# Two mixer layers on one core: bulk transfers of the second attention issued by GpSimd, and its last visits written out in a fixed order with row sums taken in the residual add

## The chip, the core and the metric

The kernel runs on one core of one Trainium2 chip. The time is the device time of one execution in microseconds (us); a kernel is timed in several runs and the median counts. A core has TensorE (PE, matrix products; PEld are its weight loads), VectorE (DVE), ScalarE (ACT), GpSimd (POOL) and SyncE (SP). Each engine works through its own queue of instructions in order and waits on semaphores for the others. TensorE writes its results to eight PSUM banks, each of 128 partitions by 512 fp32 numbers; everything else lies in SBUF, or in HBM, from and to which transfers (DMAs) run. An engine that issues a DMA only starts it, and the transfer lands later.

## The reference

Four blocks in a row, attention, token MLP, attention, token MLP, with the same weights in both rounds:

```python
    x = A_x                                            # [1, 2048, 1024], bf16
    x = x + _A_ref(_layernorm(x, axis=-1), A_wqkv, A_wo)
    x = x + _B_ref(_layernorm(x, axis=-1), B_w1, B_b1, B_w2, B_b2)
    x = x + _A_ref(_layernorm(x, axis=-1), A_wqkv, A_wo)
    x = x + _B_ref(_layernorm(x, axis=-1), B_w1, B_b1, B_w2, B_b2)
```

`_A_ref` is local dilated attention: 32 heads of 32 columns; each token attends to itself and the seven tokens before it at a distance of 2, 4, ..., 14:

```python
        qkv = x @ wqkv                                 # split into q, k, v per head
        off = jnp.arange(8) * 2
        idx = pos[:, None] - off[None, :]              # only idx >= 0 counts
        logits = jnp.einsum("bhsd,bhswd->bhsw", q, kg) * scale
        attn = softmax(where(mask, logits, -1e9))
        o = jnp.einsum("bhsw,bhswd->bhsd", attn, vg)
        return o @ wo
```

`_B_ref` is an MLP over tokens: `gelu(h^T w1 + b1) w2 + b2` with `w1` of 2048 x 3584, and `_layernorm` subtracts the row's mean and divides by the root of its variance.

## The kernel before

**Layout.** Tokens of even and odd number never attend to each other, so they are two classes c = 0, 1 of 1024 tokens, each in eight tiles i of 128. `order` lists the 16 tiles (c, i), class 0 first. `x` is kept as rows in DRAM (`xa`, `xb`), one row tile of 128 x 1024 bf16 (256 KB) per (c, i).

**The second attention** is the part that the change touches. Its q and k projections use seven products for the eight of a 2 x 2 block product (the "sevens" of the change's name, class `Attention`). One step p (there are `NP` = 8, p = 0 to 7) makes k and q for 128 columns (four heads) of one class; the weights are cut into eight blocks of 512 KB, and their sums into as many more. Before the steps, `QkBlocks` scales the blocks and forms the sums, and `keep` (L526) writes both to DRAM (`sdq`), two 512 KB stores per block; the blocks of steps 0 and 1 are used straight from SBUF (`take`). `load` (L567) reads one block and its sums back, two DMAs of 512 KB.

A step's work is given as one string per engine (L535 to L538): `P1k` ... `P7q` are the seven products for k and for q, each of four matmuls (L651); `c11q`, `c21q` (ScalarE, L712) and `y12q`, `y22q` (VectorE, L713) write the four quarters of q. `dc11q`, `dy12q`, `dy22q`, `dc21q` copy these quarters, four DMAs of 32 KB each (L667), into the padded tiles `qB`, in which each head has its own columns. `wk` and `wq` load the weights of a later step, or near the end a half of wo (`load_wo`, L742); `wx` is what is done once in a certain step: the stores of the last two blocks in step 1 (`keep_last`), the first three residual rows in step 6 (`first_rows`, through `load_xr`, L901). A name that ends in `-` belongs to the step before. `cycle` merges the strings into one program, so that each engine's order is that of its string; `chain_` fixes that order. Before the change all of these DMAs are issued by SP, in the order `dc21q- wx wk wq dc11q dy12q dy22q`.

**Visits.** Alongside step p run four visits of the attention proper over the columns of step p - 1 (16 blocks of work times two halves of tokens make 32 visits): scores `S` (L799), exp `e` on ScalarE (L807), four masks `m` that multiply the exponentials of a quarter of the partitions by a band into `Pm` (L823), values and row sums `V` (L848, L852, L861), the reciprocal in two ScalarE steps (L866, L869), and the divide `n` into `oT` (L874). The values of a visit come two visits after its scores. `V` uses two PSUM banks ("a"), which fall free with the divide.

**Output projection.** `out_proj` (L903) makes one row tile: two halves of eight matmuls (L912) in the two banks "m", on VectorE an add of the residual row for each half (L919), a store of the row, and a layer norm in three pieces (`ln_a`, `ln_b`, `ln_c`): two `bn_stats` (L930), their aggregate (L934), on ScalarE the root as a logarithm and an exponential (L208, L209), on VectorE the bias (L938), and on ScalarE the normalisation into `h2` (L952). `ln_step` issues one piece at a time after a half.

**The end of the second attention.** After the eight steps come the last visits: the rest of step 7, then four visits (`vis` from `2 * NU - 4`), in which SP, VectorE and TensorE are interleaved with `last_tile`, seven tiles in all. There, masks 2 and 3 of a visit are given to GpSimd and masks 0 and 1 to VectorE:

```python
                in_order(scores, *divmod(vis, 2))
                chain_("POOL", lambda: mask(2, 3, eng=nc.gpsimd))
                chain_("DVE", mask, 0, 1)
```

The remaining nine tiles follow in a plain loop, and then the MLP (`gemm1`; its first matmuls are L993). Its first work is on GpSimd, 32 sums and differences of `h2` tiles (`token_sums`, L1007), in the order of the tiles.

**Pools.** `wp` (nine buffers) holds weights, `gop` (14 buffers) holds `oT`, q, k, their sums and the residual rows, `vhp` (16 buffers) holds `v` and then `h2`, `x2p` (six) short-lived tiles.

Of the kernel before, what the change touches and what calls it, by code (L numbers as in the profile page):

```python
# [17 lines left out]
P = 128  # L18
# [10 lines left out]
def kernel(  # L29
# [139 lines left out]
    civ = const.tile([P, 2], FP32, name="civ")  # L169
    mx0 = const.tile([P, NPRE, DIL, NI // 2], FP32, name="mx0")  # L170
# [332 lines left out]
    class QkBlocks:  # L503
# [22 lines left out]
        def keep(self, n):  # L526
            r, t = self.R.pop(n), self.S.pop(n)
            chain_("SP", lambda: nc.sync.dma_start(out=sdq[n][0], in_=r[:].bitcast(FP16)))
            chain_("SP", lambda: nc.sync.dma_start(out=sdq[n][1].rearrange("p k c -> p (k c)"), in_=t[:].rearrange("p a k c -> p (a k c)")))

    class Attention:
# [4 lines left out]
        SP = "dc21q- wx wk wq dc11q dy12q dy22q"  # L536
# [30 lines left out]
        def load(self, phi):  # L567
            n = 2 * TURN[phi // 2 % (NG // 2)] + phi % 2
            ts = [wp.tile([P, KD, 256], FP16, name="Aq", tag="w"), wp.tile([P, 4, 4, P], FP16, name="Bq", tag="w")]
            self.w[phi] = [t[:] for t in ts]  # L570
            chain_("SP", lambda: nc.sync.dma_start(out=ts[0][:], in_=sdq[n][0]))
            chain_("SP", lambda: nc.sync.dma_start(out=ts[1][:].rearrange("p a k c -> p (a k c)"),
                                                   in_=sdq[n][1].rearrange("p k c -> p (k c)")))
# [56 lines left out]
        def cycle(self, p):  # L630
            qs = {}
            for e in ("PE", "ACT", "DVE", "SP"):
                q = [(n[:-1], p - 1) if n.endswith("-") else (n, p) for n in getattr(self, e).split()]
                qs[e] = [x for x in q if self.there(*x) and not (p == self.NP and x[1] == p)]
# [14 lines left out]
        def product(self, out, lhs, rhs, start=True):  # L649
            for k in range(4):  # L650
                r = nc.tensor.matmul(out, lhsT=lhs[:, k, :], rhs=rhs[:, k, :], start=start and k == 0, stop=k == 3,  # L651
                                     skip_group_check=True)
            return r

# [165 lines left out]
    def mask_r(pc, s0, r, eng=nc.vector):  # L820
        rp = slice(r * KG, (r + 1) * KG)
        mk = band[rp].unsqueeze(1).unsqueeze(1).to_broadcast([KG, HB, HG, GW])
        return eng.tensor_tensor(out=Pm[rp, :, s0:s0 + HB, r * KG:r * KG + GW].rearrange("p h t k -> p t h k"),  # L823
                                       in0=pc[rp], in1=mk, op=ALU.mult)

    def mask(*rs, eng=nc.vector):
        pc, s0 = exps
        for r in rs:
            mm = mask_r(pc, s0, r, eng)
# [68 lines left out]
    def load_xr(res):  # L898
        t = gop.tile([P, D], BF16, name="xr", tag="go")
        xrs.append(t)  # L900
        chain_("SP", lambda: nc.sync.dma_start(out=t[:], in_=res(*todo.pop(0))))  # L901

    def out_proj(c, i, oT, wo, res, dst, h2):  # L903
# [3 lines left out]
        xn = x2("xn")  # L907
# [9 lines left out]
        def add(n):  # L917
            xs_ = slice(n * 512, (n + 1) * 512)
            return nc.vector.tensor_tensor(out=xn[:, xs_], in0=pss_["o", n][:], in1=xr[:, xs_], op=ALU.add)  # L919

        def store():
            nc.sync.dma_start(out=rows(dst, c, i), in_=xn[:])
            h2[c][i] = vhp.tile([P, D], BF16, name="h2", tag="vh")

        t = {}

# [27 lines left out]

        return half, add, store, (ln_a, ln_b, ln_c)

    lns, late, seek = [], [], [0]
# [832 lines left out]
    for li in range(2):  # L1790
# [77 lines left out]
        else:  # L1868
# [34 lines left out]
            def keep_last():  # L1903
                for k in range(2):
                    blocks[0].keep(6 + k)

            def first_rows():
                todo[:] = order
                for _ in range(3):
                    load_xr(res)  # L1910
# [15 lines left out]
            plan = [1, 2, 2, 1, 1]  # L1926
            k = 0
            half, add, store, ln = out_proj(*order[0], oT, wo, res, xa[li], h2)
            in_order(half, 0)
            at.cycle(at.NP)  # L1930
            chain_("DVE", add, 0)
            in_order(half, 1)
            chain_("DVE", add, 1)
            store()
            lns.append(list(ln))
            in_order(values, NU - 3, 0, v, oT)
            chain_("DVE", norm.pop())
            k = 1
            for vis in range(2 * NU - 4, 2 * NU):
                in_order(scores, *divmod(vis, 2))  # L1940
                chain_("POOL", lambda: mask(2, 3, eng=nc.gpsimd))
                chain_("DVE", mask, 0, 1)
                in_order(values, *divmod(vis - 1, 2), v, oT)
                chain_("DVE", norm.pop())
                for n in range(plan[vis - 2 * NU + 5]):
                    last_tile(k, n)
                    k += 1
            in_order(values, NU - 1, 1, v, oT)
        for k, (c, i) in enumerate(order[ahead_tiles:]):
# [72 lines left out]
```

## Time and profile before

| | |
|---|---|
| Median of 3 runs | 1212.72 us (1210.88 to 1213.89) |
| The profiled execution | 1211.5 us |
| Its span, first to last instruction | 1209.8 us |
| TensorE busy | 1184.7 us (98%) |
| VectorE, ScalarE, GpSimd busy | 806.3, 731.7, 150.3 us |
| Mean granted clock of TensorE | 0.996 |
| Transfers | 197.34 MB, 56.4% of the 16 DMA engines' span, all issued from SP |

The profile gives, for each instruction, the line that issued it, its engine, and what ended its engine's idle time before it ("[6.02 <-DMA qB<-qs]": idle for 6.02 us, until a DMA into `qB` had landed). "xN" counts instructions merged into a row; a row of a timeline is start, duration, engine, line, operation. Durations of instructions in a row overlap a little, since an engine starts the next before the last has written everything. SPq rows are DMA issues on SP's queue: the time in them is that of issuing, and the chain of work has rows for the landing. The clock column is the share of full speed that TensorE was granted.

The second layer's attention lies between 606 us and 866 us of the span; its steps with k and q begin at 658 us, and its last visits end at 835 us.

### The profile page before, as it was taken

To read this page: it belongs to the slowest core of one execution; us is meant where nothing else is said; L and a number is where in the kernel's file an instruction comes from. 1 tells how busy PE (TensorE), PEld (TensorE's weight loads), DVE (VectorE), ACT (ScalarE), POOL (GpSimd) and SP (SyncE) were. 2 spreads that over 40 slices of the span, in tenths; PEclk is the share of its full clock that TensorE was granted. 3 is DMA by queue.
4 is the path that set the end of the run, shared out by engine and by line. 5 is a ranking of instruction groups with operands and counts; after the bars stand their busy time and mean duration, and the time that the engine had idled before them with its cause. 6 is when DMAs were issued, how large, how long until landed. Compare 5 with 4: busy or idle time off the path is not lost.

```text
span 1209.8 us, 20677 instructions
## 1 busy us (share of the span) xinstructions
PE 1184.7 (98%) x7908; PEld 543.5 (45%) x7908; DVE 806.3 (67%) x1533; ACT 731.7 (60%) x1220; POOL 150.3 (12%) x132
## 2 busy tenths in 40 slices
PE   9999999999999999999999799899999999999998
PEld 4444444444444444444444344444444444444444
DVE  7558887887777546866688588689633422785664
ACT  4767876678878776665667588755543434432342
POOL 0000000281000041000030000015811212100000
PEclk9999999999999999999999999999999999999999
DMA  8922233696675778966475444434967764165520
GB/s 233 160 63 71 78 105 96 211 277 167 211 201 170 209 192 194 224 178 165 123 215 203 167 164 150 156 119 139 296 182 218 215 173 149 62 191 135 154 77 35
DMA packets 257588, 197.34 MB, mean 163 GB/s; under 512 B 50128, under 2 KB 228688, under 8 KB 254160
## 3 DMA queue, kind: packets, MB, share of 16 engines
q1 hardware_dynamic: 257488, 196.01, 56.4%
q8 instruction: 62, 1.02, 0.4%
q14 instruction: 38, 0.31, 0.1%
HBM read 142.88 MB, written 38.82 MB: 150 GB/s over the span
## 4 chain that ended last, share of the span: by engine, by line
PE 87%; DMA 5%; DVE 3%; ACT 3%; SPq 1%; issue 1%; DVEq 0%; ACTq 0%
PE s L1154 11%; PE m L762 9%; PE m L912 8%; PE m L1154 7%; PE s L1363 7%; PE a L1154 6%; PE s L1513 4%; PE m L1363 4%; PE m L651 4%; PE s L299 3%; PE a L1363 3%; PE m L1513 3%; PE s L993 2%; PE s L651 2%; DMA qB<-qs 2%; PE s L449 2%
## 5 line engine op out<-in xcount | busy, mean ns | idle before, releaser
L823 DVE TENSOR_TENSOR Pm<-pc,band 32x640 bf16<-32x640 bf16 x248 | 126.2, 509 | 26.0 <-ACT pc L807 20.1
L1154 PEld LDWEIGHTS <-Sw 128*128 128x128 f16 x832 | 81.4, 98 | 99.5 <-issue 1.3
L762 PE MATMUL m<-hT,wqk 128*128 128x512 bf16 x512 | 115.9, 380 | 0.0
L912 PE MATMUL m<-wo,oT 128*128 128x512 bf16 x512 | 112.8, 379 | 3.0 <-DVE xn L919 2.2
L1154 PEld LDWEIGHTS <-w 128*128 128x128 f16 (+1 forms) x624 | 61.1, 98 | 73.6
L912 PEld LDWEIGHTS <-oT 128*128 128x128 bf16 x512 | 49.4, 98 | 64.0 <-issue 6.2
L807 ACT ACTIVATE pc<-s,shift 128x320 bf16<-128x320 f32 x128 | 62.1, 527 | 25.7 <-PE s L799 25.0
L762 PEld LDWEIGHTS <-wqk 128*128 128x128 bf16 x512 | 47.6, 98 | 59.0 <-issue 5.3
L1007 DVE TENSOR_TENSOR py<-pz,m 128x512 f32<-128x512 f32 x14 | 9.6, 687 | 86.7 <-PE m L1154 64.7
L1154 PE MATMUL s<-T,Sw 128*128 128x512 f16 x288 | 66.2, 379 | 1.1 <-ACT s L1163 1.1
L1007 POOL TENSOR_TENSOR Pm<-g 128x512 f16<-128x512 bf16 x24 | 28.6, 1207 | 286.5 <-ACT Pm L1088 164.4
L874 DVE TENSOR_TENSOR oT<-a,rd 128x512 bf16<-128x512 f32 x64 | 44.2, 691 | 25.7 <-ACT rd L869 24.3
L952 ACT ACTIVATE h<-xn,bi,rs 128x1024 bf16<-128x1024 bf16 x32 | 39.7, 1240 | 24.1 <-DVE bi L938 24.1
L1154 PE MATMUL m<-T,Sw 128*128 128x512 f16 x224 | 52.9, 379 | 0.0
L1154 PE MATMUL a<-h,w 128*128 128x512 bf16 x224 | 52.9, 379 | 0.0
L1130 ACT ACTIVATE w<-w,cs 128x2048 f16<-128x2048 bf16 x26 | 51.8, 1997 | 0.0
L919 DVE TENSOR_TENSOR xn<-m,xr 128x512 bf16<-128x512 f32 x64 | 43.9, 687 | 11.6 <-PE m L912 11.3
L1007 DVE TENSOR_TENSOR xs<-tq,xs 128x512 bf16<-128x512 f32 (+1 forms) x30 | 21.9, 732 | 44.1 <-ACT tq L1518 27.1
L1363 PEld LDWEIGHTS <-u 128*128 128x128 f16 x336 | 32.9, 98 | 39.6
L1120 DVE TENSOR_REDUCE mx<-w 128x1 f32<-128x2048 bf16 x22 | 49.2, 2275 | 0.0
L1007 POOL TENSOR_TENSOR T<-h 128x512 f16<-128x512 bf16 x16 | 18.3, 1155 | 236.8 <-ACT h L952 236.7
L1154 PE MATMUL s<-h,w 128*128 128x512 bf16 x192 | 45.4, 379 | 0.0
(294 smaller groups left out, 2418.8 us busy)
## 6 DMA issues: line engine op xcount, KB each, us to landing
w<-in_B_w_dram SPq DMA_DIRECT2D x110, 512.0 KB, 6.0
sd<-Sw SPq DMA_DIRECT2D x13, 1024.0 KB, 7.9
Sw<-sd SPq DMA_DIRECT2D x13, 1024.0 KB, 5.1
xa<-xn SPq DMA_DIRECT2D x32, 256.0 KB, 3.2
xs<-xa SPq DMA_DIRECT2D x32, 256.0 KB, 3.4
Pm<-in_B_w_dram SPq DMA_DIRECT2D x26, 256.0 KB, 6.2
Aq<-sdq SPq DMA_DIRECT2D x12, 512.0 KB, 6.0
Bq<-sdq SPq DMA_DIRECT2D x12, 512.0 KB, 6.4
```

The source lines that it names most:

```text
L651: r = nc.tensor.matmul(out, lhsT=lhs[:, k, :], rhs=rhs[:, k, :], start=start and k == 0, stop=k == 3, skip_group_check=True)
L762: mm = nc.tensor.matmul(ps[:], lhsT=wts[part][:, kt, (g % 2) * P:(g % 2 + 1) * P], rhs=hT[:, kt, lo:lo + 512], start=(kt == 0), stop=(kt = ...
L807: return nc.scalar.activation(out=pc[:, 2 * n:2 * n + 2].rearrange("p t h k -> p (t h k)"), in_=ss[n][:, 0:2 * HG * GW], func=ACT.Exp, sca ...
L823: return eng.tensor_tensor(out=Pm[rp, :, s0:s0 + HB, r * KG:r * KG + GW].rearrange("p h t k -> p t h k"), in0=pc[rp], in1=mk, op=ALU.mult)
L874: return nc.vector.tensor_tensor(out=oT[g][:, lo:lo + HB * P], in0=acc[0][:], in1=rd[:], op=ALU.mult)
L912: mm = nc.tensor.matmul(ps[:], lhsT=oT[g][:, cols(c, i)], rhs=wo[n][g // 4][:, g % 4, :], start=(g == 0), stop=(g == NG - 1))
L1007: return eng.tensor_tensor(out=out, in0=a, in1=b, op=op)
L1120: return nc.vector.tensor_reduce(out=bx[fb][:, c:c + 1], in_=w1s[fb][c][:], op=ALU.max, axis=AX.XY, apply_absolute_value=True)
L1130: return nc.scalar.activation(out=w[:].bitcast(FP16), in_=w[:], func=ACT.Identity, scale=cs[:, fb + 1:fb + 2])
L1154: r = nc.tensor.matmul(out, lhsT=lhs[:, k, :], rhs=rhs[k], start=start and k == 0, stop=stop and k == NI - 1, skip_group_check=True)
L1363: r = nc.tensor.matmul(out, lhsT=lhs[k], rhs=rhs[k][:, cols_], start=start and k == 0, stop=k == K - 1, skip_group_check=True)
L1513: r = nc.tensor.matmul(out, lhsT=lhs[k], rhs=rhs[k], start=start and k == 0, stop=k == K - 1, skip_group_check=True)
```

## The change

1. **Bulk transfers go to GpSimd's queue.** In the second attention, the loads of weight blocks (`load`), of wo (`load_wo`) and of the first three residual rows (`first_rows`) are issued by GpSimd; a queue string `POOL = "wk wq wx"` orders them. SP keeps the copies of q, and later the remaining residual rows and the stores of rows. The stores of the last two weight blocks (`keep(6)`, `keep(7)`) move from step 1 to a point ahead of step 0, and are issued by GpSimd too.
2. **The last visits in a set order.** `last_visits` writes out, engine by engine, the work from the last part of step 7 to the last visit: the tail of VectorE's and SP's strings of step 7 is cut off and placed by hand. All four masks of a visit are on VectorE. Eight tiles are projected there (seven before), and the plain loop has eight left.
3. **Row sums in the residual add.** For the eight tiles of class 0 the two adds are `tensor_tensor_reduce`, which add the residual and sum the row into `ms`; each is built as two VectorE instructions, the add and one that writes out the sum. The negative mean comes from the two sums (`mean`); ScalarE takes the sum of squares of (x - mean) (`squares`) and the root; VectorE makes the bias (`bias_m`), and ScalarE normalises in place (`norm_m`): the sum of the add is written directly into the `h2` tile, stored to DRAM from there, and overwritten with its normalised form. `bn_stats`, its aggregate and the separate row tile fall away for these tiles. Six late pieces of this are issued one by one in the plain loop (`late_steps`).

```diff
+    ms = const.tile([P, NI, 6], FP32, name="ms")
...
-        def keep(self, n):
+        def keep(self, n, e="SP"):
             r, t = self.R.pop(n), self.S.pop(n)
-            chain_("SP", lambda: nc.sync.dma_start(out=sdq[n][0], in_=r[:].bitcast(FP16)))
...
+            q = nc.sync if e == "SP" else nc.gpsimd
+            chain_(e, lambda: q.dma_start(out=sdq[n][0], in_=r[:].bitcast(FP16)))
...
-        SP = "dc21q- wx wk wq dc11q dy12q dy22q"
+        SP = "dc21q- dc11q dy12q dy22q"
+        POOL = "wk wq wx"
...
-            chain_("SP", lambda: nc.sync.dma_start(out=ts[0][:], in_=sdq[n][0]))
-            chain_("SP", lambda: nc.sync.dma_start(out=ts[1][:].rearrange("p a k c -> p (a k c)"),
...
+            chain_("POOL", lambda: nc.gpsimd.dma_start(out=ts[0][:], in_=sdq[n][0]))
+            chain_("POOL", lambda: nc.gpsimd.dma_start(out=ts[1][:].rearrange("p a k c -> p (a k c)"),
...
-                chain_("SP", lambda: nc.sync.dma_start(out=t[:], in_=wo_v[:, hf * (NG // 2):(hf + 1) * (NG // 2), n * 512:(n + 1) * 512]))
+                chain_("POOL", lambda: nc.gpsimd.dma_start(out=t[:], in_=wo_v[:, hf * (NG // 2):(hf + 1) * (NG // 2),
...
-    def out_proj(c, i, oT, wo, res, dst, h2):
+    def out_proj(c, i, oT, wo, res, dst, h2, place=False):
...
+        if place:
+            h2[c][i] = vhp.tile([P, D], BF16, name="h2", tag="vh")
+        xn = h2[c][i] if place else x2("xn")
...
         def add(n):
             xs_ = slice(n * 512, (n + 1) * 512)
+            if place:
+                return nc.vector.tensor_tensor_reduce(out=xn[:, xs_], in0=pss_["o", n][:], in1=xr[:, xs_], scale=1.0, scalar=0.0,
+                                                      op0=ALU.add, op1=ALU.add, accum_out=ms[:, i, n:n + 1])
...
+        def mean():
+            return nc.vector.tensor_scalar(out=ms[:, i, 2:3], in0=ms[:, i, 0:1], scalar1=ms[:, i, 1:2], scalar2=-1.0 / D, op0=ALU.add,
+                                           op1=ALU.mult)
+
+        def squares():
+            junk = x2("junk")
+            chain_("ACT", lambda: nc.scalar.activation(out=junk[:], in_=xn[:], func=ACT.Square, bias=ms[:, i, 2:3],
+                                                      accum_out=ms[:, i, 3:4]))
+            last["ACT"] = rsqrt(ms[:, i, 4:5], ms[:, i, 3:4], (1.0 + EPS) / D, eps2)
+
+        def bias_m():
+            return nc.vector.tensor_tensor(out=ms[:, i, 5:6], in0=ms[:, i, 2:3], in1=ms[:, i, 4:5], op=ALU.mult)
+
+        def norm_m():
+            return nc.scalar.activation(out=xn[:], in_=xn[:], func=ACT.Identity, bias=ms[:, i, 5:6], scale=ms[:, i, 4:5])
...
+    def last_visits(at, v, oT, wo, res, dst, h2):
...
+        s(5)
+        e(5)
+        va(4)
+        l(4)
+        fin(1)
+        zero_mean(3)
+        m(5, 0, 1)
+        nn(4)
+        o(4, 0)
+        a(4, 0)
+        m(5, 2, 3)
+        o(4, 1)
+        a(4, 1)
...
+        late_steps[:] = [lambda: fin(4), lambda: (bi(5), sq(6)), lambda: (fin(5), bi(6)), lambda: (sq(7), fin(6)), lambda: bi(7),
+                         lambda: fin(7)]
...
-            def keep_last():
-                for k in range(2):
-                    blocks[0].keep(6 + k)
...
-            at.late = {1: keep_last, 6: first_rows}
+            at.late = {6: first_rows}
             for k in range(2):
                 at.take(2 + k, blocks[0])
+                blocks[0].keep(6 + k, "POOL")
...
+                if p == at.NP - 1:
+                    at.DVE = at.DVE[:at.DVE.index(" y22q")]
+                    at.SP = at.SP[:at.SP.index(" dy22q")]
                 at.cycle(p)
-            ahead_tiles = 7
...
-                chain_("POOL", lambda: mask(2, 3, eng=nc.gpsimd))
-                chain_("DVE", mask, 0, 1)
...
+            ahead_tiles = 8
+            last_visits(at, v, oT, wo, res, xa[li], h2)
...
                 ln_step()
+                if late_steps:
+                    late_steps.pop(0)()
```

In `last_visits`, `s`, `e`, `m`, `va`, `l`, `nn` are scores, exp, masks, values, reciprocal and divide of visit n (2 to 7, the last six), and `o`, `a`, `zero_mean`, `sq`, `bi`, `fin` are the half projection, the summing add, the mean, the squares, the bias and the normalisation of tile k. The block shown is one visit; the others have the same shape.

More of the change, by code (lines that the diff above doesn't have):

```diff
@@ L631, in cycle @@
             qs = {}
-            for e in ("PE", "ACT", "DVE", "SP"):
+            for e in ("PE", "ACT", "DVE", "SP", "POOL"):
                 q = [(n[:-1], p - 1) if n.endswith("-") else (n, p) for n in getattr(self, e).split()]
@@ L653, in product, with one @@
             return r
+        def one(self, e, n, p):
+            if e == "PE":
+                in_order(self.do, n, p)
+            elif n[0] == "d":
+                self.do(n, p)
+            else:
+                chain_(e, self.do, n, p)
+            self.done.add((n, p))
         def place(self, f, p, a, n):
@@ L957 @@
+    late_steps = []
     lns, late, seek = [], [], [0]
```

180 lines of the change are left out of this document (147 added, 33 removed).

## The prediction

> **What bounds the kernel now.** The page first: its span and its engine row.
>
> ```profile
> span 1209.8 us, 20677 instructions
> PE 1184.7 (98%) x7908; PEld 543.5 (45%) x7908; DVE 806.3 (67%) x1533; ACT 731.7 (60%) x1220; POOL 150.3 (12%) x132
> ```
>
> TensorE is busy 98% of the span, and the change gives it the same matrix products in another order. So it can only win or lose TensorE's gaps. The profiled execution took 1211.5 us, 1.7 more than its span; the median of the three runs, 1212.72, lies 1.2 above it. The sum below is made against 1211.5.
>
> Second, TensorE's waits in the part that the change touches, 600 to 870 us (the second attention layer): columns are total us, times, longest.
>
> ```profile
> PE s L799 <- DMA qB<-qs: 11.5, 5, 6.0
> PE m L912 <- DVE xn L919: 2.2, 2, 1.7
> PE a L848 <- DVE xn L919: 1.3, 1, 1.3
> ```
>
> Two kinds: scores (L799) that wait for the copies of q into their padded tile, and, in the last visits, matmuls that wait for VectorE. Third, where they stand, in the timeline of TensorE: the fourth scores of each step from step 1 to step 7, with the two large waits in front of first scores between them, and then the first matmul of the MLP.
>
> ```profile
> 683.63 0.46 PE L799 MATMUL s<-qB,kT 128*32 128x160 bf16 x16
> 694.30 0.73 PE L799 MATMUL s<-qB,kx 128*32 128x160 bf16 x16 [6.02 <-DMA qB<-qs]
> 707.47 0.46 PE L799 MATMUL s<-qB,kx 128*32 128x160 bf16 x16
> 723.86 0.46 PE L799 MATMUL s<-qB,kT 128*32 128x160 bf16 x16
> 740.26 0.46 PE L799 MATMUL s<-qB,kx 128*32 128x160 bf16 x16
> 757.56 0.46 PE L799 MATMUL s<-qB,kT 128*32 128x160 bf16 x16
> 773.93 0.46 PE L799 MATMUL s<-qB,kx 128*32 128x160 bf16 x16
> 782.28 0.46 PE L799 MATMUL s<-qB,kT 128*32 128x160 bf16 x16 [3.68 <-DMA qB<-qs]
> 795.47 0.46 PE L799 MATMUL s<-qB,kT 128*32 128x160 bf16 x16
> 865.80 4.48 PE L993 MATMUL s<-h,w 128*128 128x512 bf16 x20
> ```
>
> The steps last 23.84, 16.39, 16.40, 17.30, 16.37 and 21.54 us. An undisturbed one lasts 16.39, with the same products and visits in it. So step 2 lost 7.45 us and step 7 5.15, more than their waits of 6.02 and 3.68: after each long wait TensorE also ran slower for a while. Step 5 lost 0.9.
>
> ```profile
> 680.00:720.00 40.00, 33.73 (x452) 16.28 (x452) 28.93 (x59) 27.67 (x52) 0.00 (x0) 0.91 0.53 183
> 717.00:733.40 16.40, 16.37 (x230) 7.79 (x229) 14.98 (x31) 13.90 (x27) 0.00 (x0) 1.00 0.47 161
> 740.26:756.65 16.39, 15.32 (x226) 7.59 (x226) 13.34 (x28) 13.07 (x26) 0.00 (x0) 1.00 0.49 170
> 797.00:835.00 38.00, 32.00 (x344) 14.91 (x343) 35.61 (x61) 18.00 (x37) 13.08 (x9) 1.00 0.37 118
> ```
>
> These stretches (us; then PE, PEld, DVE, ACT, POOL busy; granted clock; DMA share; GB/s) show a clock of 0.91 around the first long wait and 1.00 in undisturbed steps, and that in the last visits (797 to 835) VectorE is busy 35.61 of 38 us while TensorE loses 6.0.
>
> **Bulk transfers from SP to GpSimd: what it removes.** Why the q copies were late is in SP's rows (first fence: timeline of ACT and SP; second: chain of work; third: all 128 copies).
>
> ```profile
> 683.07 0.68 ACT L712 ACTIVATE qs<-s,civ 128x512 bf16<-128x512 f32 x1
> 685.10 0.42 SPq L572 DMA_DIRECT2D Bq<-sdq  x1
> 685.61 13.41 SPq L667 DMA_DIRECT2D qB<-qs  x16
> 773.37 0.68 ACT L712 ACTIVATE qs<-s,civ 128x512 bf16<-128x512 f32 x1
> 774.07 12.94 SPq L667 DMA_DIRECT2D qB<-qs  x16
> ```
> ```profile
> 687.54 6.72 DMA qB<-qs
> 776.02 6.13 DMA qB<-qs
> ```
> ```profile
> DMA to landing us min/median/max: 1.8/1.9/8.1
> ```
>
> In step 1, q was ready at 683.75, but SP issued the last weight load at 685.10 and the first copy at 685.61: 1.86 us in the queue. The copy that ended the wait then took 6.72 us to land instead of 1.9, behind four kept-weight stores and four weight loads of 512 KB (L528, L529, L571, L572). In step 6 q was ready at 774.05 and its copies started at once, but one took 6.13 us, behind three residual rows, two weight loads and two pieces of wo (L901, L571, L572, L742). Steps with only the four weight loads lost nothing, or 0.9. The change takes all of these off SP's queue in steps 1 to 7 and moves the four stores to a point before step 0, away from the copies. I take the two large losses as gone, 7.45 + 5.15 = 12.6 us, and let the small waits (step 5's 0.9, and 0.5 in step 1) stay: all of them gone would be 14.0.
>
> The row says that a copy lands late behind bulk on the same queue. The Trainium skill, "DMA: Bandwidth & Descriptors", section "Issuing engines are not separate DMA queues", says that transfers from any engine share the 16 DMA engines and that spreading them saves only issue time. By that, 1.86 us would be won and the late landings stay: a rival below. The same page, section "Queues, rings and completion order", has each DMA engine alternate between queues packet by packet, which would let 32 KB copies past 512 KB loads. No run here shows a GpSimd queue.
>
> **What it adds.** GpSimd gets 35 DMA issues: four stores, 24 weight loads, four pieces of wo, three residual rows, some four per step. Queued behind them on GpSimd is nothing but the next load until the MLP's token sums. A load has time: its buffer falls free in one step and is read in the next or the one after, more than 16.39 us later, so four issues of up to 4 us each stay hidden; beyond that TensorE's products would wait for weights. No GpSimd issue is in this trace, so what it does to VectorE is bounded: from below by nothing, from above by what GpSimd's own masks do to VectorE's (rows further down). VectorE is busy 13.34 to 14.98 of 16.39 us, so 2.2 us are free per step: 0.55 us of blocking per issue costs nothing. I take zero, because an issue moves no tile through GpSimd, and keep the mask's price for a rival.
>
> **The last visits.** Rows by line: an undisturbed stretch (707 to 774) for the first, 795 to 836 for the next five; then ScalarE's scan of w2 after the first attention (min, median, max ns), GpSimd's token sums from 797 to 870, and rows of the timeline.
>
> ```profile
> L823 DVE TENSOR_TENSOR Pm<-pc,band 32x640 bf16<-32x640 bf16 x64 | 30.8, 482 | 1.4
> ```
> ```profile
> L823 DVE TENSOR_TENSOR Pm<-pc,band 32x640 bf16<-32x640 bf16 x16 | 14.4, 899 | 0.3
> L823 POOL TENSOR_TENSOR Pm<-pc,band 32x640 bf16<-32x640 bf16 x8 | 12.2, 1529 | 197.9 <-ACT pc L807 190.9 <-DVE bn L930 6.7
> L919 DVE TENSOR_TENSOR xn<-m,xr 128x512 bf16<-128x512 f32 x14 | 9.4, 679 | 0.4 <-PE m L912 0.3
> L930 DVE BATCH_NORM_STATS2 bn<-xn 128x6 f32<-128x512 bf16 x12 | 8.2, 683 | 0.0
> L938 DVE TENSOR_SCALAR bi<-mv,rs 128x1 f32<-128x1 f32 x5 | 1.0, 208 | 0.0
> ```
> ```profile
> L1088 ACT ACTIVATE Pm<-Pm x26: 1039/1054/1061, 234.1 to 440.6; 128x1024 bf16<-128x1024 bf16 x26
> L1088 ACT ACTIVATION_READ_ACCUMULATOR Pm<-Pm x26: 185/192/194, 235.0 to 441.5; 128x1 f32 x26
> ```
> ```profile
> L1007 POOL TENSOR_TENSOR T<-h,T 128x512 f16<-128x512 bf16 x13 | 15.0, 1155 | 2.7 <-ACT h L952 2.4
> ```
> ```profile
> 802.54 1.29 DVE L919 TENSOR_TENSOR xn<-m,xr 128x512 bf16<-128x512 f32 x2
> 823.56 0.46 PE L799 MATMUL s<-qB,kx 128*32 128x160 bf16 x16
> 824.44 3.63 PE L912 MATMUL m<-wo,oT 128*128 128x512 bf16 x16
> 834.71 31.25 PE L912 MATMUL m<-wo,oT 128*128 128x512 bf16 x144
> ```
>
> A mask takes VectorE 482 ns alone. Beside GpSimd's masks the same instruction is drawn out (mean 899 over all sixteen, some of them undisturbed): in each visit VectorE is stuck for about 3.2 us in two masks that alone take 1.0. TensorE's work from 795.47 to 865.80 (70.33 us): 32 halves of the output projection at (865.80 - 834.71) / 18 = 1.73 are 55.3; a scores and its values take 824.44 - 823.56 = 0.88, five of these 4.4; two more values and two products, each under 0.9, some 2.9. Sum 62.6, so 7.7 us are lost there.
>
> After, VectorE does four masks (2.0 us, started 0.5 apart), a divide (0.6), two adds and two small instructions (208 ns, half of it beside their neighbours) per visit that carries a tile; bn_stats, two per tile at 683 ns, go. The add becomes one that also sums, followed by a read of the sum. No row has either. Its lower bound is the plain add, 0.6 start to start (two take 1.29); its upper bound an add and a second pass as long as bn_stats, 1.36. The plain add is nearest, with the same operands and shape; the read is taken at ScalarE's 0.19. So 2.0 + 0.6 + 2 x 0.8 + 2 x 0.12 = 4.4 us per visit against TensorE's 0.88 + 2 x 1.73 = 4.3: nearly even, and about 0.2 is lost in each of five visits, 1.0. GpSimd's first token sums (L1007) now start in between, as soon as a tile is normalised; with four tiles normalised early, I expect two to meet masks, at up to the 1.155 us that one takes: some 1.7. What is left of 7.7 is 5.0 (upper end 6.3, no meetings; lower end 0, sums at 1.36). ScalarE gains a squaring pass and a read per tile, 8 x (1.05 + 0.19) = 9.9 us, and had 20 us free in 797 to 835; the last two squares and four normalisations are put behind, beside the plain projection. The in-place normalisation waits for its row's store, which is issued a whole tile earlier: hidden.
>
> **Sum.** 1211.5 - 12.6 - 5.0 = 1193.9, so 1194. By their ends: 14.0 + 6.3 gives 1191; 12.6 + 0 gives 1199.
>
> **Rivals.**
> - *Same DMA engines, same lateness.* The stores do move away, but step 6's collision stays on the engines, and loads from GpSimd could hold up the copies in any step. For it: 776.02's copy was late although SP's issue was not. Against it: steps with four loads close by lost nothing. It wins 1.9 and the 5.0: 1205.
> - *The sums cost a second pass.* For it: no such instruction in the trace. Against it: the add already streams at one pass. 1199.
> - *Slower: GpSimd's issues block VectorE's masks.* For it: 482 against 899 ns, and 1529 ns for GpSimd's instruction. At 1.53 per issue, four take 6.1 of the 2.2 us free per step, 3.9 lost in each of seven steps: 27 us against a gain of 17.6, 1221. It decides from 17.6 / 28 + 0.55 = 1.2 us of blocking per issue. The Trainium skill, "SBUF — State Buffer", section "SBUF: two separate sides", makes the shared port an exclusive lock and warns that issues from GpSimd wait for VectorE; the mask rows agree on the lock, and no row here has the issue.
> - *It comes out even:* blocking near those 1.2 us, about 1212.
>
> **How the numbers follow.** Forecast 0.54, same engines 0.12, second pass 0.12, blocking 0.16, even 0.06. About 0.3% (3.6 us) is what a measurement can tell from no change. Faster holds the first three, 0.78; same 0.06; slower 0.16. The range leaves blocking out above: 1211. Below, 1191 less the runs' half spread of 1.5 is 1189. The forecast's own range is 1189 to 1199.
>
> **What would show it.** Right: scores' waits for qB under 2 us in total and all steps near 16.4, clock 1.00 there; copies landing in about 1.9; masks at 482 in the last visits; TensorE's stretch from the last fourth scores to the MLP near 65. Wrong: masks in the steps longer than 482 while GpSimd issues; products waiting for Aq or Bq; the summing add well over 0.7; TensorE waiting for xn as before.

## The result, and the profile after

The changed kernel takes 1207.39 us (median of six runs, 1205.32 to 1208.31), the kernel before beside it 1212.44 (1210.19 to 1214.0): a ratio of 0.9956 with a 95% interval of 0.9942 to 0.9971. It is 0.4% faster, and its interval lies below 1. The profiled execution took 1207.63. The forecast was 1194. The time lies inside the wide range (to 1211) and outside the forecast's own (1189 to 1199): of the 17.6 us expected, 5.0 came.

The page of the changed kernel, span and engines, and then TensorE's waits from 600 to 870 us (total us, times, longest):

```profile
span 1205.9 us, 20563 instructions
...
PE 1174.4 (97%) x7773; PEld 542.7 (45%) x7908; DVE 804.9 (67%) x1541; ACT 741.6 (61%) x1236; POOL 157.7 (13%) x159
```
```profile
PE s L812 <- DMA qB<-qs: 8.3, 3, 4.9
PE s L812 <- issue: 2.2, 3, 1.4
PE a L861 <- DVE Pm L836: 2.0, 2, 1.1
```

Scores wait 8.3 us for copies of q where they waited 11.5: the kind of wait stayed. (TensorE's busy time fell and "issue" waits appear most likely because some matmul records are missing from this trace, which has 7773 of them beside 7908 weight loads.) What is gone is every wait for xn, which belonged to the last visits. The timeline of TensorE shows where the waits went: first and fourth scores of the steps, the last fourth scores, and the first matmul of the MLP.

```profile
678.00 0.73 PE L812 MATMUL s<-qB,kT 128*32 128x160 bf16 x16 [4.86 <-DMA qB<-qs]
...
691.37 0.46 PE L812 MATMUL s<-qB,kT 128*32 128x160 bf16 x16
...
707.77 0.46 PE L812 MATMUL s<-qB,kx 128*32 128x160 bf16 x16
714.11 0.46 PE L812 MATMUL s<-qB,kT 128*32 128x160 bf16 x16 [1.70 <-DMA qB<-qs]
...
725.67 0.46 PE L812 MATMUL s<-qB,kT 128*32 128x160 bf16 x16
...
732.09 0.46 PE L812 MATMUL s<-qB,kx 128*32 128x160 bf16 x16 [1.75 <-DMA qB<-qs]
...
743.65 0.46 PE L812 MATMUL s<-qB,kx 128*32 128x160 bf16 x16
...
761.54 0.46 PE L812 MATMUL s<-qB,kT 128*32 128x160 bf16 x16
...
795.83 0.46 PE L812 MATMUL s<-qB,kT 128*32 128x160 bf16 x16
...
861.64 8.58 PE L1195 MATMUL s<-h,w 128*128 128x512 bf16 x38
```

The two stalls of before (6.02 us at 694.30, 3.68 at 782.28) are gone. A new one of 4.86 us stands a step earlier, at 678.00, and smaller ones follow (1.70 and 1.75 in the next two rows with a wait). The last fourth scores start at 795.83 where they started at 795.47: over all the steps nothing was won. From there to the MLP it takes 861.64 - 795.83 = 65.81 us where it took 70.33. These 4.5 us are the whole gain.

Why the new stall: GpSimd's rows of the timeline, and SP's row with the first copies of that step.

```profile
656.69 0.71 POOL L530 DMA_DIRECT2D sdq<-Rq  x1 [32.13 <-ACT Rq L516]
662.43 0.55 POOL L531 DMA_DIRECT2D sdq<-Sq  x1 [5.04 <-DVE Sq L1209]
...
664.47 0.54 POOL L574 DMA_DIRECT2D Aq<-sdq  x1
...
669.62 0.54 POOL L575 DMA_DIRECT2D Bq<-sdq  x1 [1.43 <-PE m L654]
```
```profile
669.24 134.82 SPq L679 DMA_DIRECT2D qB<-qs  x124
```

Four stores and eight loads of 512 KB, 6 MB, leave GpSimd, all but the first store between 662.43 and 670.16 us, because nothing in its queue stands between them; only the last load waits, 1.43 us for a matmul. The first copies of q are issued at 669.24, beside the last of them. The stretches from 669 to 692 (columns: PE, PEld, DVE, ACT, POOL busy; granted clock; DMA share; GB/s), and the copy that ended the wait, from the chain of work:

```profile
669.00:678.00 9.00, 3.89 (x18) 1.53 (x18) 2.65 (x7) 2.69 (x5) 0.54 (x1) 0.94 1.01 373
678.00:683.80 5.80, 5.80 (x28) 2.04 (x28) 0.00 (x0) 1.51 (x3) 0.00 (x0) 0.50 0.64 206
684.00:692.00 8.00, 7.79 (x122) 3.95 (x120) 6.93 (x13) 6.33 (x13) 0.00 (x0) 1.00 0.01 2
```
```profile
671.79 6.08 DMA qB<-qs
```

The DMA engines are full at 373 GB/s, and a 32 KB copy takes 6.08 us to land. All copies of q from 600 to 870 us have a median of 3.0 us, where it was 1.9:

```profile
DMA to landing us min/median/max: 1.8/3.0/6.7
```

Behind the wait TensorE runs at half speed for a while (granted clock 0.50 from 678 to 683.8 us, 1.00 from 684 on), so the stall costs more than its 4.86 us, as both stalls of before did.

### The profile page after: what moved, and what is told of

Its sections match the earlier page's. It is cut to its first block, busy times and chain, and to the rows that moved or that the text cites. A ratio compares the mean times of both kernels' runs of the same rounds, so it can differ in the third digit from the quotient of the medians.

```text
span 1205.9 us, 20563 instructions
## 1 busy us (share of the span) xinstructions
PE 1174.4 (97%) x7773; PEld 542.7 (45%) x7908; DVE 804.9 (67%) x1541; ACT 741.6 (61%) x1236; POOL 157.7 (13%) x159
## 4 chain that ended last, share of the span: by engine, by line
PE 88%; DMA 5%; ACT 2%; DVE 2%; issue 2%; SPq 1%; DVEq 0%; ACTq 0%
PE s L1356 11%; PE m L775 9%; PE m L927 8%; PE m L1356 7%; PE s L1565 7%; PE a L1356 6%; PE s L1715 5%; PE m L1565 4%; PE m L654 4%; PE a L1565 3%; PE s L654 3%; PE m L1715 3%; PE s L1195 2%; PE s L300 2%; PE s L450 2%; PE s L1808 2%
## 5 line engine op out<-in xcount | busy, mean ns | idle before, releaser
L775 PE MATMUL m<-hT,wqk 128*128 128x512 bf16 x481 | 111.8, 379 | 3.1 <-issue 2.2
L1371 ACT ACTIVATE g<-pz,b_sb,ci 128x512 bf16<-128x512 f32 x26 | 21.1, 813 | 36.4 <-DVE pz L1209 36.4
L1209 DVE TENSOR_TENSOR py<-pz,s 128x512 f32<-128x512 f32 x12 | 8.3, 688 | 52.8 <-PE s L1356 43.7
```

The lines of the kernel that those rows point to most:

```text
L775: mm = nc.tensor.matmul(ps[:], lhsT=wts[part][:, kt, (g % 2) * P:(g % 2 + 1) * P], rhs=hT[:, kt, lo:lo + 512], start=(kt == 0), stop=(kt = ...
L1209: return eng.tensor_tensor(out=out, in0=a, in1=b, op=op)
```

## The experiments

Two theories were set against each other. **A, the moment:** all transfers share the 16 DMA engines; a copy of q is late when megabytes were issued just ahead of it, whichever engine issued them. SP's queue, in which loads stood behind the copies of the step before, had set a good moment nearly everywhere; GpSimd's queue, with nothing between its loads, sets worse ones. **B, the queue:** transfers from GpSimd's queue delay SP's copies by themselves.

**The two halves of the change.** First the last visits alone, with all bulk left on SP as before:

```
-        SP = "dc21q- dc11q dy12q dy22q"
-        POOL = "wk wq wx"
+        SP = "dc21q- wx wk wq dc11q dy12q dy22q"
...
-            at.late = {6: first_rows}
+            at.late = {1: keep_last, 6: first_rows}
```

> Only the last visits are changed (set order, sums in the add); all bulk transfers stay on SP, in the order and at the places of before. Theory A (the bulk's moment decides: all transfers share the DMA engines, and GpSimd's queue, which nothing paces, issues its bulk at worse moments than SP did) and theory B (a bulk transfer from GpSimd's queue delays SP's copies of q by itself, more than the same transfer from SP's queue would) say the same here: the waits of scores for qB are those of before, about 11.5 us in 600 to 870 us, and the last visits win 4.5 us as in the changed kernel: 1208 us, ratio 0.996. If the last visits win less than 3 us here, the bulk on SP's queue delays the residual rows or row stores of the last visits, and part of the gain belongs to the move.

Then the queues alone, the same edit the other way round in the kernel before:

```
-        SP = "dc21q- wx wk wq dc11q dy12q dy22q"
+        SP = "dc21q- dc11q dy12q dy22q"
+        POOL = "wk wq wx"
```

> Only the bulk transfers are moved to GpSimd (with the early stores of the last two weight pairs); the last visits are those of before, with GpSimd's masks. Both theories: the two large waits of before go and the new ones of the changed kernel come (about 4.9 us in step 1, 1.7 us in each of steps 3 and 4), so the move alone is worth about nothing: 1212 us, ratio 1.000 within 0.002. Were it 1207 or less, the move would have won and the last visits would have lost.

The last visits alone took 1205.64 us, ratio 0.9962 (0.9947 to 0.9976); the queues alone 1208.63, ratio 0.9990 (0.9977 to 1.0003). All ratios are to the kernel before timed beside the run, here 1210.1 us. The product is 0.9952, the whole change 0.9956: the two parts add up, the visits carry the gain, and the move of the queues cannot be told from nothing. Scores' waits for qB, first of the visits alone, then of the queues alone:

```profile
PE s L811 <- DMA qB<-qs: 11.4, 6, 6.6
```
```profile
PE s L801 <- DMA qB<-qs: 7.5, 4, 4.2
```

**Moments set by hand, on either queue.** One kernel keeps the bulk on GpSimd and holds each step's loads back with a small copy that needs the step's last quarter of q:

```
-        POOL = "wk wq wx"
+        POOL = "G1- wk wq wx"
...
+            if n == "G1":
+                return nc.gpsimd.tensor_copy(out=ms[:, NI - 1, 5:6], in_=self.qs[:, 2, 511:512])
```

> The changed kernel, but GpSimd first copies one column of q's last quarter before each step's loads, so that its loads are issued only when the step's last quarter of q is ready, where SP issued them before; the early stores stay. Theory A: step 1 loses nothing (7.45 us won), steps 3 to 5 lose at most 0.5 us each (some 4 us won), waits of scores for qB below 2 us in total: 1195.5 us, ratio to before 0.986. Theory B: the loads still run beside the copies and delay them; only the burst of 6 MB is thinner: 1202 to 1207 us, ratio 0.992 to 0.996.

The other has all bulk on SP, in before's places, except for the transfers that were in the way: the stores go ahead of the first step, the residual rows to step 7.

```
-        SP = "dc21q- dc11q dy12q dy22q"
-        POOL = "wk wq wx"
+        SP = "dc21q- wk wq wx dc11q dy12q dy22q"
...
-            at.late = {6: first_rows}
+            at.late = {7: first_rows}
...
-                blocks[0].keep(6 + k, "POOL")
...
             at.load(4)
+            for k in range(2):
+                blocks[0].keep(6 + k)
```

> The changed last visits; all bulk on SP again, between the steps' copies as before, but the four stores of the last two weight pairs stand ahead of the first step and the three residual rows in step 7 behind wo, away from the copies that were late. Theory A: both large waits go without any second queue, 12.6 us, and the last visits' 4.5 come on top: 1195.5 us, ratio 0.986, equal to the paced GpSimd queue within 2 us. Theory B: also about 1195.5, but then better than the paced GpSimd queue by 6 us or more. If a second queue is what lets copies pass bulk, this one stays at 1200 or above while the paced GpSimd queue is faster.

All on SP: 1194.2 us, ratio 0.9860 (0.9838 to 0.9883), the time that theory A gave within 1.3 us. That is 11.4 us below the last visits alone, so most of the 12.6 us was there to be won, and no second queue was needed. The gated GpSimd queue: 1203.15, ratio 0.9937 (0.9915 to 0.9960), as theory B had it. But my gate stood at a worse moment than SP's: q's last quarter being ready does not mean that its copies are issued. GpSimd's rows of the timeline show the gate and the loads behind it:

```profile
690.12 0.46 POOL L693 CAST ms<-qs 128x1 f32<-128x1 bf16 x1 [16.87 <-ACT qs L728]
690.62 0.54 POOL L574 DMA_DIRECT2D Aq<-sdq  x1
691.15 0.54 POOL L575 DMA_DIRECT2D Bq<-sdq  x1
696.11 0.54 POOL L574 DMA_DIRECT2D Aq<-sdq  x1 [4.42 <-PE m L656]
```

By SP's pace in the all-SP kernel (16 copies in 11.85 us, in a row further down) the step's copies are still being issued at 690.62, when the first of these loads goes out beside them, and the second pair waits for a buffer until 696.11. Queue and moment differ at once, so this run does not decide. (Its profile is of its fastest execution, 1198.24 us of 1198.24 to 1206.62, and shows less lost time than the median has.)

**The same moment on both queues, twice.** In the kernel with the schedule of the all-SP one, GpSimd waits for the landing of the step's last copy:

```
+            if n == "G1":
+                return nc.gpsimd.tensor_copy(out=ms[3 * DH:P, NI - 1, 5:6], in_=qB[1][3 * DH:P, 3, 511:512])
```

> The schedule of the all-SP kernel (early stores, rows in step 7, loads behind each step's last copy), but the bulk is issued by GpSimd: before each step's loads it copies one column of what the step's last copy of q brought, so that the loads are issued when that copy has landed, some 2 us later than SP issued them. Theory A (the moment decides, not the queue): waits of scores for qB 2 to 5 us in total, 1195.5 us, within 2.5 us of the all-SP kernel's 1194.2, ratio to before 0.985 to 0.989. Theory B (GpSimd's transfers delay SP's copies by themselves): copies land later than in the all-SP kernel at every step, 1200 us or more, ratio over 0.990.

It took 1202.81 us, ratio 0.9932 (0.9908 to 0.9957): theory A's number missed by 7 us. But the loads were also issued some 2 us later than SP's in the all-SP kernel. Two kernels separate the two. One gives SP's queue that later moment:

```
-        SP = "dc21q- wk wq wx dc11q dy12q dy22q"
+        SP = "dc21q- G1- wk wq wx dc11q dy12q dy22q"
...
+            if n == "G1":
+                return nc.sync.dma_start(out=ms[3 * DH:P, NI - 1, 5:6].bitcast(BF16), in_=qB[1][3 * DH:P, 3, 510:512])
```

> The all-SP kernel, but SP first waits, by a transfer of 32 x 2 values that reads what the step's last copy brought, until that copy has landed, and issues the step's loads then: the same queue, some 2 us later, the moment at which GpSimd issued them in the kernel gated by the landing. Theory A (the moment decides): scores wait about 11 us for qB in total, as there, and it takes about 1202 us, ratio 0.993. Theory B (GpSimd's queue by itself makes the copies late): the wait stays under 6 us and the time under 1198.

The other gives GpSimd's queue the earlier one, by the landing of the first of the last four copies:

```
-                return nc.gpsimd.tensor_copy(out=ms[3 * DH:P, NI - 1, 5:6], in_=qB[1][3 * DH:P, 3, 511:512])
+                return nc.gpsimd.tensor_copy(out=ms[0:DH, NI - 1, 5:6], in_=qB[1][0:DH, 0, 511:512])
```

> The kernel whose GpSimd queue is gated by the landing, but by that of the first of the last four copies in place of the fourth: about 2 us earlier, near the moment at which SP issued the loads in the all-SP kernel. Theory A: scores wait 2 to 6 us for qB in total, 1194 to 1198 us, ratio 0.986 to 0.989. Theory B: 1200 us or more, ratio over 0.990.

| loads issued by | moment of the first load of step 1 | after the kernel's first copy of q, us | scores' wait for qB, us | time, us | ratio |
|---|---|---|---|---|---|
| SP | 676.34 | 10.1 | 4.5 | 1194.2 | 0.9860 (0.9838 to 0.9883) |
| GpSimd | 676.20 | 10.0 | 5.5 | 1196.21 | 0.9893 (0.9878 to 0.9908) |
| GpSimd | 678.33 | 12.0 | 11.1 | 1202.81 | 0.9932 (0.9908 to 0.9957) |
| SP | 679.76 | 12.0 | 9.8 | 1202.53 | 0.9947 (0.9927 to 0.9967) |

The rows behind the table, in its order: for each kernel the first copies of q and the first load, from the timeline of SP or GpSimd (for SP with the copies that follow), and then scores' wait, from TensorE's waits.

```profile
666.20 10.04 SPq L678 DMA_DIRECT2D qB<-qs  x16
676.34 0.53 SPq L573 DMA_DIRECT2D Aq<-sdq  x1
...
681.32 11.85 SPq L678 DMA_DIRECT2D qB<-qs  x16
```
```profile
PE s L811 <- DMA qB<-qs: 4.5, 7, 2.1
```
```profile
666.18 125.70 SPq L681 DMA_DIRECT2D qB<-qs  x124
...
676.20 0.53 POOL L574 DMA_DIRECT2D Aq<-sdq  x1 [0.34 <-DMA qB<-qs]
```
```profile
PE s L816 <- DMA qB<-qs: 5.5, 8, 1.9
```
```profile
666.30 133.74 SPq L681 DMA_DIRECT2D qB<-qs  x119
...
678.33 0.54 POOL L574 DMA_DIRECT2D Aq<-sdq  x1 [0.19 <-PE s L816]
```
```profile
PE s L816 <- DMA qB<-qs: 11.1, 6, 3.3
```
```profile
667.79 10.04 SPq L680 DMA_DIRECT2D qB<-qs  x16
...
679.76 0.53 SPq L573 DMA_DIRECT2D Aq<-sdq  x1
...
683.17 11.29 SPq L680 DMA_DIRECT2D qB<-qs  x16
```
```profile
PE s L815 <- DMA qB<-qs: 9.8, 6, 2.3
```

The moment decides: SP's queue at the later moment loses as much as GpSimd's, and GpSimd's at the earlier one wins nearly what SP's does. The two GpSimd kernels differ by the one line above and by 6.6 us. (The profiled executions of the two kernels with the later moment took 1206.57 and 1206.54 us, 3.8 and 4.0 above their medians, so the median execution may wait less than their rows show.) Between the issue of 2 MB in step 1 and the next copies the all-SP kernel has 681.32 - 676.34 = 5.0 us; delayed, 683.17 - 679.76 = 3.4, and that is too little. All six steps of the delayed SP kernel agree: four with 3.3 to 3.9 us between loads and copies are followed by waits of 2.0 to 2.3 us in front of the next step's first scores, two with 5.2 and 5.8 by none. An estimate fits: at the 373 GB/s of the full stretch above, the four loads, 2.1 MB, take 5.6 us, 2.2 more than 3.4. The first two rows lie 2.0 us apart, but their intervals overlap, so it is not shown that a queue of its own costs anything beyond the moment. Theory B, which gave 1200 or more for GpSimd at the earlier moment, falls.

**The burst on SP's queue.** The all-SP kernel, with 6 MB issued by SP ahead of the first copies:

```
                 blocks[0].keep(6 + k)
+            for k in range(3):
+                at.load(5 + k)
...
+                if phi < 8:
+                    return
```

> The all-SP kernel with the changed kernel's burst put back: the four early stores and then the loads of four weight pairs' halves (6 MB in all with the one already under way) are issued by SP ahead of the first copies of q; the loads of later steps as in the all-SP kernel. Theory A: the first scores of step 1 wait about 4.9 us, as they did with the burst on GpSimd's queue, and with the slower TensorE behind it some 7 us are lost: 1201. Theory B: the burst on SP's queue costs less than half of that, under 1198.

It took 1200.5 us in the one run, 6.3 above the all-SP median (5.4 if each is counted from the kernel before beside it, 1211.02 and 1210.1); A said 1201. The wait is there again on the other queue, a little longer than the 4.86 of the changed kernel:

```profile
676.68 0.73 PE L813 MATMUL s<-qB,kT 128*32 128x160 bf16 x16 [5.52 <-DMA qB<-qs]
```

**One transfer more out of the way.** In the all-SP kernel the step with half of its loads from wo still waited 2.13 us; one of the wo halves goes a step later:

```
-            for hf in range(2):
+            for n, hf in ([(0, 0)] if n == 0 else [(0, 1), (1, 0), (1, 1)]):
```

> The all-SP kernel with one more transfer moved: the second half of the first piece of wo (0.5 MB) goes from step 6, where scores still waited 2.13 us and TensorE ran 2.4 us late, to step 7. Theory A: 1.5 MB ahead of step 6's copies in place of 2, the wait falls under 0.7 us, and about 2 us are won: 1192.2 us, ratio 0.9845. Theory B says nothing of it. If the wait stays, it is not the amount in front of the copies.

That step's wait is gone in the trace, and the wait for qB falls to 1.7 us in all. The time is 1193.8 us, ratio 0.9850 (0.9829 to 0.9872): against the all-SP kernel the intervals overlap, and the 2 us expected are not shown.

**What won the last visits.** The prediction named masks drawn out beside GpSimd's, and the statistics. Each was undone alone, the set order kept. Masks 2 and 3 of the last four visits back on GpSimd:

```
-                chain_("DVE", mask_r, pcs[n][0], (z + n) % NS * HB, r)
+                chain_("DVE" if r < 2 else "POOL", mask_r, pcs[n][0], (z + n) % NS * HB, r, nc.vector if r < 2 else nc.gpsimd)
```

> The all-SP kernel with the last four visits' masks 2 and 3 back on GpSimd, everything else in the set order. If it is the masks drawn out beside GpSimd's that cost the last visits their time: VectorE is held some 3.2 us in two masks in place of 2.0 in four, 1.2 us in each of four visits, and the stretch from the last fourth scores to the MLP grows from 65.8 to about 70 us. If the set order won it: under 67.5.

The sums apart, with a plain add:

```
-                return nc.vector.tensor_tensor_reduce(out=xn[:, xs_], in0=pss_["o", n][:], in1=xr[:, xs_], scale=1.0, scalar=0.0,
...
+            stat_half(0)
+            stat_half(1)
+            return aggregate()
```

> The all-SP kernel with the first eight tiles' sums taken apart again: a plain add, two bn_stats of 683 ns and an aggregation per tile on VectorE, no squares on ScalarE, in the same set order. If the sums in the add matter, VectorE has some 1.2 us more per tile than the 4.3 us of TensorE's visit allow, in five visits, and the stretch from the last fourth scores to the MLP grows from 65.8 to about 71 us. If VectorE has room: under 67.5.

Neither came near 70 us, so both were undone together, and the masks' edit was put on the kernel with wo split:

> The all-SP kernel with masks 2 and 3 of the last four visits on GpSimd and the sums apart: of the changed last visits only the set order stays. If the order alone won the 4.5 us: the stretch from the last fourth scores to the MLP stays at 64.5 to 67.5 us (each of the two undone alone gave 64.5 and 67.1). If either of the two parts can stand in for the other, and one of them is needed: 69 to 71 us, as in the kernel before (70.3).

> The kernel with wo split over two steps, and masks 2 and 3 of the last four visits on GpSimd in the set order, which alone made the stretch to the MLP 64.5 in place of 65.8 us. Both add up: 1.3 us below the split kernel's 1193.8, about 1192.5, ratio 0.984. If the 1.3 us were those of one execution, it stays at 1193.8, ratio 0.985.

The stretch from the last fourth scores to the MLP, worked out from the timeline's rows. Three of these four kernels have one execution each, but the stretch repeats: it is 65.81 to 65.85 us in the traces of nine kernels that share the changed last visits, and 70.33 and 70.35 in the two that have those of before.

| set order with | masks all on VectorE | masks 2 and 3 on GpSimd |
|---|---|---|
| sums in the add | 850.25 - 784.44 = 65.81 | 848.41 - 783.89 = 64.52 |
| sums apart | 847.96 - 780.87 = 67.09 | 852.65 - 784.30 = 68.35 |

Rows of both undone, with TensorE's wait for the add, and then of the kernel with wo split and the masks back (which also has 64.52):

```profile
784.30 0.46 PE L811 MATMUL s<-qB,kT 128*32 128x160 bf16 x16
...
852.65 0.59 PE L1190 MATMUL s<-h,w 128*128 128x512 bf16 x2
```
```profile
PE m L926 <- DVE h L933: 2.3, 4, 1.8
```
```profile
781.00 0.46 PE L811 MATMUL s<-qB,kT 128*32 128x160 bf16 x16
...
845.52 0.81 PE L1194 MATMUL s<-h,w 128*128 128x512 bf16 x3
```

Against 70.33 before, the set order with both undone is worth 2.0 us, and in it are the eighth tile and the normalisation in place, which were not undone; this fits neither expectation, it lies between them. The sums in the add are worth 1.3 us with the masks on VectorE and 3.8 with them on GpSimd. Taking the masks off GpSimd won 1.3 us only while the sums were apart; with the sums in the add it cost 1.3. VectorE's and GpSimd's groups from 784 to 850 us in the kernel with masks back and sums in the add:

```profile
L835 DVE TENSOR_TENSOR Pm<-pc,band 32x640 bf16<-32x640 bf16 x16 | 12.1, 758 | 1.7 <-ACT pc L819 1.5
...
L835 POOL TENSOR_TENSOR Pm<-pc,band 32x640 bf16<-32x640 bf16 x8 | 12.8, 1598 | 180.3 <-ACT pc L819 180.0
```

VectorE's masks are drawn out there to 758 ns on average, and the stretch is still the shorter one. VectorE has the room with the sums in the add (busy 30.34 of 38 us, behind PE and PEld in the row of 785 to 823 us):

```profile
785.00:823.00 38.00, 37.31 (x371) 17.32 (x370) 30.34 (x74) 28.55 (x54) 17.28 (x12) 1.00 0.42 130
```

The 2.0 us that values wait for VectorE's masks in the changed kernel (Pm in its first waits) are not among this kernel's. They come from GpSimd's token sums; rows of the changed kernel, in which one starts just before two masks:

```profile
818.04 1.15 POOL L1209 TENSOR_TENSOR T<-h 128x512 f16<-128x512 bf16 x1 [3.94 <-ACT h L961]
818.18 1.86 DVE L836 TENSOR_TENSOR Pm<-pc,band 32x640 bf16<-32x640 bf16 x2
...
820.10 0.42 PE L861 MATMUL a<-Pm,v 128*32 128x136 bf16 x16 [0.85 <-DVE Pm L836]
```

The two masks take 1.86 us where two take 0.97 elsewhere, and the values wait 0.85; at 827.91 us it is the same again, with 1.13. With masks 2 and 3 on GpSimd the token sums stand behind these: the first starts at 816.77 us, after VectorE's last mask has started at 813.8, and none meets one.

The kernel with wo split and masks back has the lowest median of all, 1191.91 us (1191.21 to 1192.8), where 1192.5 was expected. But its ratio, 0.9854 (0.9838 to 0.9871), is that of the kernel with wo split alone (0.9850): the kernel before took 1209.58 beside the one and 1211.02 beside the other. The 1.3 us show in the stretch, and not in the time.

## Why the prediction was wrong, step by step

- **Where the time is lost before:** right. With the late copies out of the way the all-SP kernel took 1194.2 us, and the step terms, 7.45 and 5.15, together were of the right size.
- **"I take the two large losses as gone, 7.45 + 5.15 = 12.6 us":** this step failed. The losses at their old places went; new ones came. Step 1 lost 7.0 us: from the moment its first scores were due, 678.00 - 4.86 = 673.14, to the fourth at 691.37 it took 18.23, and 11.19 before (from 672.44, in the timeline of before, to 683.63). The six steps from there to 795.83 took 104.46 us in place of 6 x 16.39 = 98.34, 6.1 lost; three of them are 17.90 (707.77 to 725.67), 17.98 (to 743.65) and 17.89 (to 761.54). Together 13.1 us, nearly what before had lost (7.45 + 0.9 + 5.15 = 13.5). The prediction moved "the four stores to a point before step 0, away from the copies" without asking what else would be issued there. With SP's order gone, eight loads followed the stores, all but the last at once. "Queued behind them on GpSimd is nothing but the next load" was true, and this was the fault: a queue without anything to wait for has no moment of its own.
- **The reading "behind bulk on the same queue":** wrong in the words "on the same queue". The copy that ended the new wait took 6.08 us to land with all bulk on another queue, and the median copy after 3.0 where it had been 1.9. The rival built on shared DMA engines (1205, chance 0.12) came nearest to the measured time. It had cited the rule: the Trainium skill, "DMA: Bandwidth & Descriptors", section "Issuing engines are not separate DMA queues", says that transfers share the 16 DMA engines whoever issues them. The four rows of the table agree with it. The page's rule of alternation packet by packet, on which the forecast leaned, did not keep 32 KB copies from landing after 6.08 us here; no run shows whether it holds on a single engine. That the rival's time came near was in part luck: it left the late landings at their old places and won 1.9, the queueing ahead of them; in the trace the old places lost nothing, and 13.1 us were lost at new ones.
- **GpSimd's issues cost VectorE nothing:** right. An issue takes 0.54 us on GpSimd, and from 691.37 to 761.54 us, beside 14 such issues, masks take what they took:

```profile
L836 DVE TENSOR_TENSOR Pm<-pc,band 32x640 bf16<-32x640 bf16 x64 | 30.8, 482 | 1.3
```

  The rival of blocking (1221) falls. So does, for this case, the fear that it drew from the Trainium skill, "SBUF — State Buffer", section "SBUF: two separate sides", that GpSimd's issues wait for VectorE: from 664 to 790 us the two kinds of weight load land in a median of 4.0 and 4.8 us from GpSimd at the earlier moment, 3.9 and 4.4 in the all-SP kernel.
- **The last visits, 5.0:** 4.5 in the trace, and the ratio of the visits alone is worth the same (0.0038 x 1210.1 = 4.6). The size was right, the account in part wrong: I explained the lost time by drawn-out masks, and they cost nothing once the sums are in the add. Two token sums that meet masks, "some 1.7", were foreseen rightly, at 2.0. The order was given no term of its own and, with the eighth tile and the normalisation in place, holds 2.0 us. Two steps of the working do not come out: 4.44 against 4.34 is 0.1 us per visit and not 0.2, and the upper end without meetings is 7.7 - 1.0 = 6.7 and not 6.3; the first moves the forecast by 0.5, the second only the lower end of its range. The summing add was sized well and its read too high, at 82 ns against 190 taken:

```profile
L935 DVE CUSTOM_DVE_ANT_0 h<-m,xr x16: 680/687/692, 799.8 to 834.2; 128x512 bf16<-128x512 f32 x16
L935 DVE DVE_READ_ACCUMULATOR2_ANT ms<- x16: 81/82/84, 800.4 to 834.8; 128x1 f32 x16
```

  The rival of a second pass for the sums (1199) falls with these rows: the add takes 687 ns where the plain one took 679.

## What to carry to other kernels

A queue in which transfers stand behind other work is also a clock for them. Before bulk is moved to a queue of its own, ask what will hold each transfer back there, and put the list of issue moments beside the moments at which small urgent copies are due; an idle queue issues everything as soon as a buffer is free. Where a small copy is late behind bulk, move the bulk in time, not to another engine: here the same last visits took 1207.4 us with the second queue and 1194.2 with a new order on the old one, and loads issued some 2 us later in each step, on either queue, cost 6.6 to 8.3 us.

## What the runs showed of the hardware that was not expected

- A stall on TensorE has a tail: behind 4.86 us of waiting the granted clock was 0.50 for the next 5.8 us and then 1.00 again, and the step lost 7.0.
- The accumulator's read on VectorE, 82 ns, is less than half of ScalarE's (186 ns in the changed kernel's squares, 192 before).
- Masks drawn out from 482 to 758 ns on average beside GpSimd's did not lengthen a stretch in which VectorE had room; it was 1.3 us shorter than with four masks on VectorE, where two token sums of GpSimd, 1.15 us each, drew masks out and cost waits of 2.0 us.
